# A fixed order on ScalarE and a fourth staging buffer in an attention and two-MoE kernel

## The chip, the cores and the metric

The kernel runs on one core of a Trainium2 chip. The metric is the device time of one execution in microseconds (us). A core has five engines that run their own instruction streams in order and meet through semaphores: TensorE (PE, matrix products and transposes; its weight loads are PEld), VectorE (DVE), ScalarE (ACT), GpSimd (POOL) and SyncE (SP, which issues most transfers).

## What is computed

Three stages, all in fp32: attention in a band of 64 positions (4 batches, 8 heads, 576 positions, head size 64), a dense layer pair with a squared relu (MoE1), and a layer pair for which each token picks one of eight experts (MoE2). Cut to what matters:

```python
scores = where((rel >= 0) & (rel < 64), q @ k.T / 8, -1e9)
x = (softmax(scores) @ v).reshape(2304, 512)

h = maximum(x @ w_in, 0)                 # 512 -> 2048
x = (h * h) @ w_out                      # 2048 -> 512

logits = x @ w_gate + modality_bias[modality_id]
e_idx = argmax(logits, 1); gate_w = softmax(logits)[e_idx]
for e in range(8):                       # tokens with e_idx == e
    out[mask] = gate_w * (maximum(x[mask] @ w1[e], 0) @ w2[e])   # 512 -> 1024 -> 512
```

## The kernel before

**Arithmetic.** An fp32 product is made of three matmul passes over operands that are split into a high and a low part: high by high, high by low, low by high. For every operand ScalarE makes the high part by a cast or by the activation itself (`xh` L769, `hh` L498 and L519, weights `w` L432) and VectorE the low part by a subtraction (`xl` L770, `hl` L506 and L520, weights L435). A matmul therefore waits for ScalarE first and for VectorE next.

**Steps.** `run` (L807 on) drives a job in steps. A step is one slice of the hidden layer: `emit_L1` issues its first-layer matmuls (L480), `evac_L1` brings the result from the accumulator to `hh` and `hl`, and then `emit_L2` issues the second-layer matmuls (L539) of the step before. In MoE1 `evac_L1` is a relu to `hr` (L492), a square to `hh` (L498), another square in place (L503) and the subtraction `hl`; in MoE2 it is one relu to `hh` (L519) and `hl`. Twice in a step `run` calls a `work` function, which inserts other work: half steps are numbered s = 0, 1, 2 and so on.

**Stages.** A hand-written program covers the attention and the first MoE1 groups. The last MoE1 group (512 tokens, 16 steps) is run with `last_work`. Then come units of 256 rows of MoE2: 0, 1 and 2 for the *guessed expert*, whose share of the first 14 token tiles is known early, then 3, a unit "w" of 384 rows, and 4 to 7. Units 0 and 1 have work functions of their own; from unit 2 on a loop over `seq` uses `u_work`.

**Weights.** `dma_chunks` (L391 on, the transfer at L399) lets SP load a 128 by 512 chunk (256 KB) of an expert's weights into a staging tile `st`; `split_steps` issues the cast of a chunk (L432), the subtraction of the chunk before, and the load of one more chunk. Sixteen chunks make a unit's weights. Staging has `nb` buffers (pool "stage2") for the guessed expert, issued in the last MoE1 group from half step `lsp` on, and `nb2` (pool "stage3") for those after it, whose memory is that of the gate's pool and so comes free after unit 1. The list `sp` says how many chunks are split in each half step of a unit.

**Gate.** `gate_steps` (L548 on) is done for each tile of 128 tokens. A copy `x` of MoE1's accumulator (L728, ScalarE) feeds eight dot products on VectorE (L559), the logits `nl` (L563), an exponential `lg` on ScalarE (L565), two small matmuls `ps_r` for the token's place in its expert's list, a scatter of the token's number into the table `tbl` (L588, POOL) and the write of its row to `xs` (L591, POOL). `slot(n)` issues the next n pieces of this and other background work.

**Rows of a unit.** `gather` reads a piece of the table into `ix` (L745), and POOL gathers the rows that it names (L751). `transp` transposes them on TensorE into `ps_x` (L310), from which `xh` and `xl` are made. At a unit's end ScalarE and VectorE scale the result `o` (L788, L790), and POOL scatters it to the output (L792).

**What sets the order.** The file fixes what is issued, but a scheduler chooses the order in which each engine meets its instructions, by times that it works out itself. It may move a weight cast ahead of an evacuation that the file has earlier, on any engine, within what data and buffers allow. Engines keep to the order chosen, however late one of its inputs may be.

Of the kernel before, what the change touches and what calls it, by code (L numbers as in the profile page):

```python
# [1 line left out]
KN = {'at1': ((0, 3, 4, 5), (3, 6, 7, 8), (6, 9, 10, 11), (9, 12, 13, 14)),  # L2
# [4 lines left out]

# [6 lines left out]
FP32 = mybir.dt.float32  # L14
F32R = mybir.dt.float32r
BF16 = mybir.dt.bfloat16
I32 = mybir.dt.int32
# [37 lines left out]
def kernel(  # L55
# [14 lines left out]
    nc = tc.nc  # L70
    NT, DM = out.shape
    E = w1.shape[0]
    NG = NT // 64
    NTT = NT // 128
# [9 lines left out]
    ROW = DM + 1  # L84
# [3 lines left out]
    const = ctx.enter_context(tc.tile_pool(name="const", bufs=1))  # L88
# [3 lines left out]
    small = ctx.enter_context(tc.tile_pool(name="small", bufs=2))  # L92
    dram = ctx.enter_context(tc.tile_pool(name="dram", bufs=1, space=DRAM))
    bank_p = ctx.enter_context(tc.tile_pool(name="bank", bufs=8, space=PSUM))
    att_ctx = ExitStack()
    att = att_ctx.enter_context(tc.tile_pool(name="att", bufs=2, side="right"))
    att2_ctx = ExitStack()
    att2 = att2_ctx.enter_context(tc.tile_pool(name="att2", bufs=1, side="right"))
    conv_ctx = ExitStack()
    conv = conv_ctx.enter_context(tc.tile_pool(name="conv", bufs=2))  # L100
    gp = {}
# [3 lines left out]
    tbl = dram.tile([NSLOT, 1], I32, name="tbl")  # L105

    ident = const.tile([128, 128], FP32, name="ident")
    maskn = const.tile([128, 128], FP32, name="maskn")
    mask_lo = const.tile([128, 128], FP32, name="mask_lo")
    mask_hi = const.tile([128, 128], FP32, name="mask_hi")  # L110
    upper = const.tile([128, 128], BF16, name="upper")
    ones = const.tile([128, 128], BF16, name="ones")
    row0 = const.tile([128, 128], BF16, name="row0")
# [70 lines left out]

    def setup_bias():
        nc.sync.dma_start(out=biasb, in_=mbias.partition_broadcast(128))
        modi = small.tile([128, NTT, 2], I32, tag="modi", name="modi", bufs=1)
        nc.sync.dma_start(out=modi, in_=mod)
        m1 = small.tile([128, NTT], FP32, tag="m1", name="m1", bufs=1)
        m0 = small.tile([128, NTT], FP32, tag="m0", name="m0", bufs=1)  # L190
        nc.vector.tensor_copy(m1, modi[:, :, 0])
        nc.vector.tensor_scalar(out=m0, in0=m1, scalar1=-1.0, scalar2=1.0, op0=ALU.mult, op1=ALU.add)
        tb = gp["x2"].tile([128, ROW], FP32, tag="x2", name="x2", bufs=4)[:, 0:NTT * E]
        tb = tb.rearrange("p (t e) -> p t e", e=E)
        for dst, m, r in ((bsel, m1, 1), (tb, m0, 0)):
            nc.vector.tensor_tensor(
                out=dst,
                in0=m.unsqueeze(2).to_broadcast([128, NTT, E]),
                in1=biasb[:, r, :].unsqueeze(1).to_broadcast([128, NTT, E]),
                op=ALU.mult,  # L200
            )
        nc.vector.tensor_tensor(out=bsel, in0=bsel, in1=tb, op=ALU.add)
# [3 lines left out]
    PRE = 6  # L206
# [3 lines left out]
    def home(kind, j):  # L210
        mine = held[kind]
        if j not in mine:
            mine[j] = att2 if j < PRE and not any(p is att2 for p in mine.values()) else att
        return mine[j]

    def load_qk(j):
# [174 lines left out]
    def dma_chunks(n):  # L391
        for _ in range(min(n, len(pend_dma))):
            key, c, f0, src = pend_dma.pop(0)
            w = src.shape[1]
            if len(src.shape) == 3:
                st = conv.tile([128, 512, 4], U16, tag="st", name="st", bufs=4)[:, 0:w, :]
            else:
                st = stage[0].tile([128, 512], FP32, tag="st", name="st", bufs=8 if stage[0] is conv else None)[:, 0:w]
            nc.sync.dma_start(out=st, in_=src)  # L399
            pend_split.append((key, c, f0, st))  # L400
# [28 lines left out]
    def split_hi(where, src):  # L429
        if where[0] not in units:  # L430
            units[where[0]] = ring.tile([128, 2, 4, 512], F32R, tag="w", name="w")
        nc.scalar.copy(out=part(where, 0, src), in_=src)  # L432

    def split_lo(eng, where, src):
        eng.tensor_tensor(out=part(where, 1, src), in0=src, in1=part(where, 0, src).bitcast(FP32), op=ALU.subtract)  # L435
        key, c, f0 = where
        done.update((key, c, f) for f in range(f0, f0 + src.shape[1], 256))

    def split_steps(n):
        for _ in range(n):  # L440
            if not pend_split and not pipe:
                return
            if pipe:
                split_lo(nc.vector, *pipe.pop())
            if pend_split:
                key, c, f0, st = pend_split.pop(0)
                pipe.append(((key, c, f0), st))
                split_hi(*pipe[0])
            dma_chunks(1)

    def add_expert(u, ev):
        for f in range(2):
            add_unit((u, "a", f), [
                w1[bass.ds(ev, 1), 128 * kk:128 * (kk + 1), 512 * f:512 * (f + 1)].rearrange("o p f -> (o p) f")
                for kk in range(4)])
            add_unit((u, "b", f), [
                w2[bass.ds(ev, 1), 512 * f + 128 * c:512 * f + 128 * (c + 1), :].rearrange("o p d -> (o p) d")
                for c in range(4)])
# [241 lines left out]
        yield  # L700


    bg = []

    def slot(n=1):
        for g in list(bg):
            while n > 0:
                try:
                    n -= 1
                    if next(g):  # L710
                        break
                except StopIteration:
                    n += 1
                    bg.remove(g)
                    break
# [22 lines left out]
    def gather(u, base, n):  # L738
        assert state["n"] >= (GUESS_TT if u in range(GUESS) else NTT)
        nh = 3 if u == "w" else 2  # L740
        sfx = "w" if u == "w" else ""
        pool = gp["wide"] if u == "w" else late["row"]
        ix = late["row"].tile([128, nh], I32, tag="ix" + sfx, name="ix" + sfx, bufs=1 if u == "w" else 3)
        eng = nc.gpsimd if u in range(GUESS) else nc.sync
        eng.dma_start(out=ix, in_=tbl[bass.ds(base, 128 * nh), :].rearrange("(h p) o -> p (h o)", p=128))  # L745
        r = []
        for hf in range(nh):
            t = pool.tile([128, ROW], FP32, tag="row", name="row")
            nc.gpsimd.memset(t, 1.0)
            ia = ix[:, hf:hf + 1].bitcast(U32)  # L750
            nc.gpsimd.indirect_dma_start(  # L751
                out=t[:, :], out_offset=None, in_=xs[0:n, :],
                in_offset=bass.IndirectOffsetOnAxis(ap=ia, axis=0),
                bounds_check=n - 1, oob_is_err=False)
            r.append((t, ia))
        rows[u] = r
# [96 lines left out]
    order = list(pend_dma)  # L853
# [99 lines left out]
    stage[0] = ctx.enter_context(tc.tile_pool(name="stage2", bufs=KN["nb"], side="right"))  # L953
    add_expert(0, ev0)

    def last_work(s):
        if s == 0:
            dma_chunks(KN["nb"])
        if s >= KN['lsp']:
            split_steps(1)  # L960
        slot(2)
        for u, at in enumerate(KN['lg']):
            if s == at:
                gather(u, bv0 + 256 * u, 128 * GUESS_TT)
# [31 lines left out]
    def prep(u):  # L996
        if u == "w":
            ew, bw = wei[0:1, 0:1], wbi[0:1, 0:1]
        else:
            ew, bw = ewi[0:1, u - GUESS:u - GUESS + 1], bsi[0:1, u - GUESS:u - GUESS + 1]  # L1000
        ev = nc.sync.value_load(ew, min_val=0, max_val=E - 1)
        evs[u] = nc.sync.value_load(bw, min_val=0, max_val=NSLOT - WIDE)
        add_expert(u, ev)
# [6 lines left out]
    def u_work(i, wide):  # L1010
        nxt = seq[i + 1] if i + 1 < len(seq) else None

        def f(s):
            if nxt is None or (wide and s % 2):
                return
            s = s // 2 if wide else s
            if s == KN['g']:
                gather(nxt, evs[nxt], NT)
            split_steps(KN['sp'][s])
            if s == KN['prep'] and i + 2 < len(seq):  # L1020
                prep(seq[i + 2])
                dma_chunks(KN["nb2"])
        return f

    def u_pieces(i, wide):
        def f(s):
            if i + 1 < len(seq) and s == (KN['tw_'] if wide else KN['t0'] if i == 0 else KN['t']):
                transp(seq[i + 1])
        return f

    for i, u in enumerate(seq):
        run(moe2_job(u), u_work(i, u == "w"), u_pieces(i, u == "w"), u == seq[-1])

    tot = nc.values_load(toti[0:1, 0:1], min_val=0, max_val=LIST)  # L1034

    def extra(u):
# [64 lines left out]
```

## Time and profile before

| | |
|---|---|
| median of 3 runs | 747.83 us (747.26 to 748.58) |
| profiled execution, its own time | 749.85 us |
| its span | 748.2 us |
| mean granted TensorE clock | 0.970 |
| TensorE busy | 700.5 us, 94% |
| VectorE, ScalarE, GpSimd busy | 448.2, 357.2 and 89.7 us (60%, 48%, 12%) |
| DMA | 84.49 MB in 62412 packets, mean 113 GB/s |

The times of the rows below are of the profiled execution, counted from its start. A wait is idle time of an engine together with what ended it. The granted clock is a share of TensorE's full 2.4 GHz. Busy time of matmuls is modelled and counts a slow matmul as busy too, so the loss behind a drop of the clock does not show as idle time. In this execution the last MoE1 group runs to about 508 us, unit 0 to about 531, unit 1 to about 554, and from there unit 2 and the rest follow.

### The profile page before, as it was taken

The numbers are of one execution on the slowest core, as the hardware profiler recorded it, in microseconds if no ns is written. First come the engines' busy times: TensorE is split into PE (matmuls) and PEld (weight loads), VectorE is DVE, ScalarE is ACT, GpSimd is POOL, SyncE is SP. The second block draws the span as 40 slices with busy tenths as digits, with TensorE's granted clock in tenths as the row PEclk, the third lists the DMA queues.
The fourth block names the chain that finished last, engine by engine and source line by source line (L and its number), as shares of the span: only waits on it lengthen the run. The fifth ranks groups of instructions, "written<-read, shape, count | busy, mean of one in ns | idle before, by whom it ended". The sixth has DMA issues, their size and how long they took to land. (4 is left out here: it accounts for less than half of the span.)

```text
span 748.2 us, 13360 instructions
## 1 busy us (share of the span) xinstructions
PE 700.5 (94%) x4777; PEld 599.1 (80%) x4777; DVE 448.2 (60%) x1394; ACT 357.2 (48%) x841; POOL 89.7 (12%) x126
## 2 busy tenths in 40 slices
PE   6499999999999999999999969799968999999995
PEld 5498888888888888788888757588868999999994
DVE  3999995597657433975446753118847765466311
ACT  5877667554444444553444333334106754456310
POOL 3000000000000000010001010400323321122111
PEclk7799999999999999999999999899988999999999
DMA  8976632435312203241201358400139874576200
GB/s 228 277 243 212 191 125 62 152 109 125 62 31 64 78 30 51 63 71 26 75 29 57 57 99 52 104 0 15 43 64 298 289 237 141 169 249 225 64 29 20
DMA packets 62412, 84.49 MB, mean 113 GB/s; under 512 B 26016, under 2 KB 35248, under 8 KB 62208
## 3 DMA queue, kind: packets, MB, share of 16 engines
q1 hardware_dynamic: 57136, 69.26, 34.9%
q0 software_dynamic: 5200, 14.29, 5.9%
q8 instruction: 39, 0.64, 0.4%
q14 instruction: 37, 0.30, 0.2%
HBM read 74.23 MB, written 9.82 MB: 112 GB/s over the span
## 5 line engine op out<-in xcount | busy, mean ns | idle before, releaser
L480 PE MATMUL l<-xh,w 128*128 128x256 f32 (+2 forms) x1344 | 318.2, 320 | 8.1 <-ACT xh L769 8.1
L539 PE MATMUL acc<-w,hh 128*128 128x512 f32 x880 | 280.4, 399 | 9.7 <-ACT hh L498 9.7
L480 PEld LDWEIGHTS l<-xh,w 128*128 128x128 f32 x1344 | 227.9, 191 | 27.9 <-ACT xh L769 8.8
L480 PE MATMUL l<-xl,w 128*128 128x256 f32 (+2 forms) x672 | 213.2, 317 | 0.0
L539 PEld LDWEIGHTS acc<-w,hh 128*128 128x128 f32 x880 | 161.9, 191 | 41.7 <-ACT hh L498 11.6
L539 PE MATMUL acc<-w,hl 128*128 128x512 f32 x440 | 174.5, 397 | 4.6 <-DVE hl L506 4.6
L480 PEld LDWEIGHTS l<-xl,w 128*128 128x128 f32 x672 | 128.4, 191 | 9.2 <-DVE xl L770 0.2
L539 PEld LDWEIGHTS acc<-w,hl 128*128 128x128 f32 x440 | 83.8, 190 | 26.1 <-DVE hl L506 8.2
L435 DVE TENSOR_TENSOR w<-st,w 128x512 fp32r<-128x512 f32 x112 | 72.3, 686 | 52.8 <-ACT w L432 52.7
L492 ACT ACTIVATE hr<-l 128x512 f32<-128x512 f32 x72 | 42.7, 593 | 122.1 <-PE l L480 108.7
L559 DVE CUSTOM_DVE_ANT_0 junk<-x,wgb 128x512 bf16<-128x512 f32 x144 | 98.9, 687 | 2.9 <-ACT x L728 0.4
L506 DVE TENSOR_TENSOR hl<-hr,hh 128x512 fp32r<-128x512 f32 x72 | 49.7, 690 | 83.0 <-ACT hr L503 82.6
L432 ACT CAST w<-st 128x512 fp32r<-128x512 f32 x112 | 64.2, 621 | 62.7 <-DMA st<-in_moe_w_dram 51.1
L277 ACT ACTIVATE p<-p,nm 128x128 f32<-128x128 f32 x144 | 55.9, 390 | 26.0 <-DVE nm L268 26.0
L519 ACT ACTIVATE hh<-l 128x512 fp32r<-128x512 f32 (+1 forms) x40 | 23.1, 577 | 82.8 <-PE l L480 76.4
L520 DVE SCALAR_TENSOR_TENSOR hl<-l,hh 128x512 fp32r<-128x512 f32 (+1 forms) x40 | 26.4, 660 | 53.0 <-ACT hh L519 52.9
L591 POOL DMA_DIRECT2D xs<-x x18 | 10.3, 572 | 308.0 <-PE ps_o L355 150.1
L498 ACT ACTIVATE hh<-hr 128x512 fp32r<-128x512 f32 x72 | 45.5, 631 | 3.2 <-PE acc L539 1.4
L503 ACT ACTIVATE hr<-hr 128x512 f32<-128x512 f32 x72 | 45.4, 631 | 1.7
L588 POOL DMA_INDIRECT tbl<-tid,pi x18 | 19.6, 1087 | 167.5 <-DVE pi L585 121.6
L310 PE MATMUL ps_t<-ident,p 128*128 128x128 f32 x144 | 23.6, 290 | 12.0 <-DVE p L302 9.0
L268 DVE CUSTOM_DVE_ANT_0 p<-ps_s,maskn 128x128 f32<-128x128 f32 x112 | 24.9, 285 | 11.9 <-POOL tri L175 6.4
(146 smaller groups left out, 559.6 us busy)
## 6 DMA issues: line engine op xcount, KB each, us to landing
st<-in_moe_w_dram SPq DMA_DIRECT2D x112, 256.0 KB, 4.0
vt<-in_v_dram SPq DMA_DIRECT2D x35, 256.0 KB, 3.8
st<-in_moe_w_out_dram SPq DMA_DIRECT2D x16, 512.0 KB, 3.7
kt<-in_k_dram SPq DMA_DIRECT2D x17, 384.0 KB, 3.9
st<-in_moe_w_in_dram SPq DMA_DIRECT2D x12, 512.0 KB, 4.9
xs<-x POOLq DMA_DIRECT2D x18, 256.5 KB, 3.8
qt<-in_q_dram SPq DMA_DIRECT2D x36, 128.0 KB, 4.4
st<-in_moe_w_in_dram SPq DMA_DIRECT2D x8, 256.0 KB, 5.2
```

The costliest lines, as they stand in the source:

```text
L268: nc.vector.tensor_tensor_reduce(out=p[:, pr, :], in0=ps[:, pr, :], in1=mk, scale=-SCALE, scalar=3.0e38, op0=ALU.add, op1=ALU.min, accum_o ...
L277: nc.scalar.activation(out=p[:, pr, :], in_=p[:, pr, :], func=ACTF.Exp, scale=-1.0, bias=nm[:, pr:pr + 1], accum_out=sm[:, pr:pr + 1])
L432: nc.scalar.copy(out=part(where, 0, src), in_=src)
L435: eng.tensor_tensor(out=part(where, 1, src), in0=src, in1=part(where, 0, src).bitcast(FP32), op=ALU.subtract)
L480: nc.tensor.matmul(out=ps[:, job.cols * j:job.cols * (j + 1)], lhsT=wt[:, a, kk, f0:f0 + 128], rhs=job.x[b][:, kk, :], start=(kk == 0 and ...
L492: nc.scalar.activation(out=e["r"], in_=ps, func=ACTF.Relu)
L498: nc.scalar.activation(out=e["hh"], in_=e["r"], func=ACTF.Square)
L503: nc.scalar.activation(out=e["r"], in_=e["r"], func=ACTF.Square)
L506: nc.vector.tensor_tensor(out=hl, in0=e["r"], in1=e["hh"].bitcast(FP32), op=ALU.subtract)
L520: nc.vector.scalar_tensor_tensor(out=hl, in0=ps, scalar=0.0, in1=hh.bitcast(FP32), op0=ALU.max, op1=ALU.subtract)
L539: nc.tensor.matmul(out=job.acc[th], lhsT=h[a][:, c0:c0 + 128], rhs=wt[:, b, c, :], start=(mp == 0 and j == 0 and n == 0), stop=(mp == last ...
L559: nc.vector.tensor_tensor_reduce(out=gp["junk"], in0=x2[:, 0:DM], in1=gp["wgb"][:, e, :], scale=1.0, scalar=0.0, op0=ALU.mult, op1=ALU.add ...
```

## The change

1. **Order.** The new functions `settle` and `skip` chain instructions of ScalarE to each other in the order of the file, by dependences that need no semaphore. The chain covers what is issued after `add_expert(0, ev0)`, that is from the last MoE1 group to the end of the loop over `seq`. The other engines are still ordered by the scheduler.
2. **Staging.** `nb` is 4 instead of 3. To make room, the masks of the attention move from the pool that lives throughout to one that ends with the attention.
3. **Pace.** Casts of the guessed expert begin at half step 8 instead of 7, and `last_work` issues one piece of background work instead of two from there on. The gathers of units 0 to 2 (`lg`) are two half steps later. From unit 2 on the casts are spread over all half steps (`sp0` for unit 2, `sp` for the others); the next unit but one is announced (`prep`) at half step 2 instead of 7, without loads at that place.
4. **Memory of the start.** The tile of the modality numbers shares a gate tile, which puts its load behind another one, and the value tiles of pair 4 and 5 change pools (`home`).

The core of the diff (list entries that stay are left out):

```diff
-      ... 'lsp': 7, 'lg': [20, 22, 24], ...
-      ... 'sp': [3, 3, 4, 4, 1, 3, 2, 0], 'nb': 3, 'nb2': 6, 'rb': 6, 'prep': 7, ...
+      ... 'lsp': 8, 'lg': [22, 24, 26], ...
+      ... 'sp0': [0, 1, 2, 2, 2, 3, 3, 4], 'sp': [2, 2, 2, 2, 2, 2, 2, 3], 'nb': 4, 'nb2': 6, 'rb': 6, 'prep': 2, ...
...
+    maskn, mask_lo, mask_hi = (att.tile([128, 128], FP32, name=n, bufs=1) for n in ("maskn", "mask_lo", "mask_hi"))
...
-    maskn = const.tile([128, 128], FP32, name="maskn")
-    mask_lo = const.tile([128, 128], FP32, name="mask_lo")
-    mask_hi = const.tile([128, 128], FP32, name="mask_hi")
...
-        modi = small.tile([128, NTT, 2], I32, tag="modi", name="modi", bufs=1)
+        tb = gp["x2"].tile([128, ROW], FP32, tag="x2", name="x2", bufs=4)
+        m1, m0 = (tb[:, NTT * k:NTT * (k + 1)] for k in (E, E + 1))
+        modi = tb[:, NTT * (E + 2):NTT * (E + 4)].bitcast(I32).rearrange("p (t w) -> p t w", w=2)
...
-            mine[j] = att2 if j < PRE and not any(p is att2 for p in mine.values()) else att
+            mine[j] = att2 if j < PRE and j != PRE - 2 and not any(p is att2 for p in mine.values()) else att
...
+    def settle(*engines):
+        made = nc.cur_bb.bb.instructions
+        for i in made[seen[0]:]:
+            if i.engine in engines:
+                if i.engine in tail:
+                    tc.add_manual_dep(i, tail[i.engine], mybir.DependencyInfo(
+                        mybir.DependencyClass.NoSync, mybir.DependencyReason.DATA), reason="order of the file")
+                tail[i.engine] = i.name
+        seen[0] = len(made)
+
+    def skip():
+        seen[0] = len(nc.cur_bb.bb.instructions)
+        tail.clear()
...
+    skip()
+    PINNED = (mybir.EngineType.Activation,)
...
-        slot(2)
+        slot(2 if s < KN['lsp'] else 1)
...
-            split_steps(KN['sp'][s])
+            split_steps(KN['sp' if i else 'sp0'][s])
             if s == KN['prep'] and i + 2 < len(seq):
                 prep(seq[i + 2])
-                dma_chunks(KN["nb2"])
...
+    settle(*PINNED)
```

Three places on ScalarE, the kernel before and the changed kernel one after the other. Line numbers of the changed kernel are its own: L489, L495 and L500 are relu, `hh` and second square, L429 the weight cast, L742 the copy of an accumulator, L562 the exponential, L516 the relu of MoE2, L783 `xh`, L802 the output scaling. First, the last MoE1 group where the casts of the guessed expert begin, before:

```order
L492 ACTIVATE hr<-l_4790 128x512
L432 CAST w<-st 128x512
L498 ACTIVATE hh<-hr 128x512
L432 CAST w<-st 128x512
L503 ACTIVATE hr<-hr 128x512
L432 CAST w<-st 128x512 x2
L492 ACTIVATE hr<-l_4846 128x512
L498 ACTIVATE hh<-hr 128x512
L565 ACTIVATE lg,gs<-nl,gm 128x8
L503 ACTIVATE hr<-hr 128x512
L432 CAST w<-st 128x512 x3
L492 ACTIVATE hr<-l_4904 128x512
```

and changed:

```order
L489 ACTIVATE hr<-l_4789 128x512
L495 ACTIVATE hh<-hr 128x512
L500 ACTIVATE hr<-hr 128x512
L429 CAST w<-st 128x512
L489 ACTIVATE hr<-l_4841 128x512
L495 ACTIVATE hh<-hr 128x512
L500 ACTIVATE hr<-hr 128x512
L429 CAST w<-st 128x512 x2
L489 ACTIVATE hr<-l_4895 128x512
L495 ACTIVATE hh<-hr 128x512
L500 ACTIVATE hr<-hr 128x512
L429 CAST w<-st 128x512 x2
```

Casts that stood between the relu, `hh` and the second square of a step now stand behind all three, one at first and then two for each step.

Second, the end of the last MoE1 group and unit 0, where `x` copies the accumulators of MoE1 for the gate, before:

```order
L769 CAST xh<-ps_x 128x4x128 x2
L728 COPY x_5449<-acc 128x512
L728 COPY x_5454<-acc 128x512
L519 ACTIVATE hh<-l_5417 128x512
L728 COPY x_5459<-acc 128x512
L728 COPY x_5464<-acc 128x512
L565 ACTIVATE lg,gs<-nl,gm 128x8
L519 ACTIVATE hh<-l_5481 128x512
L769 CAST xh<-ps_x 128x4x128 x2
L519 ACTIVATE hh<-l_5564 128x512
L565 ACTIVATE lg,gs<-nl,gm 128x8
```

and changed:

```order
L783 CAST xh<-ps_x 128x4x128 x2
L516 ACTIVATE hh<-l_5414 128x512
L742 COPY x_5446<-acc 128x512
L742 COPY x_5451<-acc 128x512
L742 COPY x_5456<-acc 128x512
L742 COPY x_5461<-acc 128x512
L562 ACTIVATE lg,gs<-nl,gm 128x8
L516 ACTIVATE hh<-l_5478 128x512
L783 CAST xh<-ps_x 128x4x128 x2
L562 ACTIVATE lg,gs<-nl,gm 128x8
L516 ACTIVATE hh<-l_5561 128x512
```

All four copies went behind the first `hh` of unit 0, and the second exponential went from behind the third `hh` to ahead of it.

Third, from unit 1 to unit 2, before:

```order
L519 ACTIVATE hh<-l_5861 128x512
L519 ACTIVATE hh<-l_5920 128x512
L432 CAST w<-st 128x512 x2
L769 CAST xh<-ps_x 128x4x128 x2
L432 CAST w<-st 128x512 x2
L788 ACTIVATE o<-acc,row 128x512
L432 CAST w<-st 128x512 x4
L519 ACTIVATE hh<-l_6031 128x512
```

and changed:

```order
L516 ACTIVATE hh<-l_5858 128x512
L516 ACTIVATE hh<-l_5917 128x512
L783 CAST xh<-ps_x 128x4x128 x2
L516 ACTIVATE hh<-l_6028 128x512
L802 ACTIVATE o<-acc,row 128x512
L429 CAST w<-st 128x512 x3
L516 ACTIVATE hh<-l_6095 128x512
L429 CAST w<-st 128x512 x4
```

The casts for unit 3 moved from both sides of `xh` to behind `xh`, the first `hh` of unit 2 and the output scaling.

## Rows read from the trace of the kernel before

**Rows 1.** Stages, core 0: window, its length, busy time (instructions) of each engine, granted clock, DMA share, GB/s

```profile
421.00:480.00 59.00, 46.00 (x182) 34.57 (x181) 24.82 (x78) 21.36 (x41) 11.79 (x13) 0.91 0.66 81
480.00:505.00 25.00, 25.00 (x112) 20.68 (x111) 2.77 (x4) 8.61 (x14) 1.50 (x2) 1.00 0.11 31
...
553.00:570.00 17.00, 8.88 (x47) 7.63 (x46) 6.19 (x10) 6.37 (x12) 3.52 (x6) 0.70 0.69 184
```

**Rows 2.** TensorE's waits, 420 to 480: total us, times, longest

```profile
PE acc L539 <- ACT hh L498: 9.7, 4, 4.7
PE acc L539 <- DVE hl L506: 3.3, 4, 1.3
```

**Rows 3.** Timeline of TensorE in the last MoE1 group: start, us, instruction, idle time before

```profile
413.00 0.39 PE L480 MATMUL l<-xh,w 128*128 128x512 f32 x1
...
447.18 0.73 PE L539 MATMUL acc<-w,hh 128*128 128x512 f32 x2 [3.84 <-ACT hh L498]
...
487.06 0.39 PE L480 MATMUL l<-xh,w 128*128 128x512 f32 x1
...
503.38 0.39 PE L480 MATMUL l<-xh,w 128*128 128x512 f32 x1
```

**Rows 4.** ScalarE's waits, 420 to 480

```profile
ACT w L432 <- DMA st<-in_moe_w_dram: 30.9, 6, 8.5
```

**Rows 5.** Timeline of ScalarE in the last MoE1 group

```profile
443.40 0.62 ACT L432 CAST w<-st 128x512 fp32r<-128x512 f32 x1 [8.46 <-DMA st<-in_moe_w_dram]
...
446.50 0.63 ACT L498 ACTIVATE hh<-hr 128x512 fp32r<-128x512 f32 x1
```

**Rows 6.** Timeline of TensorE between units 1 and 2

```profile
553.33 1.04 PE L310 MATMUL ps_x<-ident,row 128*128 128x128 f32 x8
...
563.41 0.58 PE L480 MATMUL l<-xh,w 128*128 128x256 f32 x1 [8.12 <-ACT xh L769]
```

**Rows 7.** Timeline of ScalarE between units 1 and 2

```profile
561.21 1.18 ACT L432 CAST w<-st 128x512 fp32r<-128x512 f32 x2 [9.84 <-DMA st<-in_moe_w_dram]
562.29 1.07 ACT L769 CAST xh<-ps_x 128x512 fp32r<-128x512 f32 x2
```

**Rows 8.** The table by stage (columns as in rows 1) behind the second hole

```profile
557.30:567.50 10.20, 4.09 (x14) 3.61 (x15) 5.08 (x9) 5.81 (x11) 1.88 (x3) 0.50 0.83 234
```

**Rows 9.** Weight loads (L399) issued in 399-416, 447-458 and 420-475

```profile
DMA to landing us min/median/max: 2.9/2.9/3.0
...
DMA to landing us min/median/max: 11.2/12.2/13.1
...
DMA to landing us min/median/max: 2.6/7.8/13.1
```

**Rows 10.** Timeline of POOL in the last MoE1 group

```profile
447.78 1.01 POOL L588 DMA_INDIRECT tbl<-tid,pi  x1 [0.31 <-issue]
457.99 1.03 POOL L588 DMA_INDIRECT tbl<-tid,pi  x1 [9.20 <-issue]
```

**Rows 11.** Timeline of ScalarE in unit 0

```profile
508.10 0.59 ACT L728 COPY x<-acc 128x512 f32<-128x512 f32 x1
...
522.21 0.60 ACT L519 ACTIVATE hh<-l 128x512 fp32r<-128x512 f32 x1 [2.15 <-PE ps_r L575]
523.35 0.30 ACT L565 ACTIVATE lg<-nl,gm 128x8 f32<-128x8 f32 x1 [0.54 <-DVE gm L563]
```

**Rows 12.** Timeline of TensorE in unit 0, the first L2 matmul of its third step

```profile
527.73 0.71 PE L539 MATMUL acc<-w,hh 128*128 128x512 f32 x2
```

**Rows 13.** Timeline of POOL, third row gather for unit "w"

```profile
590.68 1.02 POOL L751 DMA_INDIRECT row<-xs,ixw  x1 [0.30 <-issue]
```

**Rows 14.** Timeline of TensorE, transposes for unit "w"

```profile
604.32 1.47 PE L310 MATMUL ps_x<-ident,row 128*128 128x128 f32 x12
```

**Rows 15.** Weight loads (L399) issued in 553 to 700

```profile
DMA to landing us min/median/max: 2.4/3.9/6.4
```

**Rows 16.** ScalarE's waits, 553 to 748

```profile
ACT w L432 <- DMA st<-in_moe_w_dram: 20.2, 13, 9.8
```

More of the change, by code (lines that the diff above doesn't have):

```diff
@@ L186, in setup_bias @@
         nc.sync.dma_start(out=biasb, in_=mbias.partition_broadcast(128))
-        modi = small.tile([128, NTT, 2], I32, tag="modi", name="modi", bufs=1)
+        tb = gp["x2"].tile([128, ROW], FP32, tag="x2", name="x2", bufs=4)
+        m1, m0 = (tb[:, NTT * k:NTT * (k + 1)] for k in (E, E + 1))
+        modi = tb[:, NTT * (E + 2):NTT * (E + 4)].bitcast(I32).rearrange("p (t w) -> p t w", w=2)
         nc.sync.dma_start(out=modi, in_=mod)
-        m1 = small.tile([128, NTT], FP32, tag="m1", name="m1", bufs=1)
-        m0 = small.tile([128, NTT], FP32, tag="m0", name="m0", bufs=1)
         nc.vector.tensor_copy(m1, modi[:, :, 0])
         nc.vector.tensor_scalar(out=m0, in0=m1, scalar1=-1.0, scalar2=1.0, op0=ALU.mult, op1=ALU.add)
-        tb = gp["x2"].tile([128, ROW], FP32, tag="x2", name="x2", bufs=4)[:, 0:NTT * E]
-        tb = tb.rearrange("p (t e) -> p t e", e=E)
+        tb = tb[:, 0:NTT * E].rearrange("p (t e) -> p t e", e=E)
         for dst, m, r in ((bsel, m1, 1), (tb, m0, 0)):
@@ L700, in list_steps @@
         yield
+    seen, tail = [0], {}
+    def settle(*engines):
[10 more added lines that the diff above has]
+        tail.clear()
     bg = []
```

4 rows, old and new, of the table KN are left out of this document.

## The prediction

> **What bounds the kernel now.** I read the table by stage first, then TensorE's waits in the stages where its busy time falls short of the stretch, then the engine that those waits name. From 480 to 505 us TensorE is busy the whole time at full clock; in the two stretches 421 to 480 and 553 to 570 it is busy 46.00 of 59.00 us at a mean clock of 0.91 and 8.88 of 17.00 us at 0.70 [rows 1]. Between them and after them TensorE waits for nothing that the list of waits shows. So the kernel is bound by TensorE, with two holes in it, and a change that only moves ScalarE's work and weight loads can be worth those holes and no more.
>
> *The first hole.* TensorE waits there for `hh` (9.7 us) and for `hl` (3.3 us), the two halves of MoE1's hidden tile [rows 2]. How much the hole costs in all is better read from the pace than from the waits, since the clock falls too. The last matmul of L1 starts at 413.00 in the third step of the last group and at 503.38 in the last, thirteen steps later; the last three steps, which are free of waits, take (503.38 - 487.06) / 3 = 5.44 us each [rows 3]. Thirteen such steps are 70.7 us, the rows give 90.4: **19.7 us** are lost. What ScalarE did meanwhile: six times it stood before a cast of the guessed expert's weights whose staged tile had not landed, 30.9 us in all [rows 4]. One such place shows the link: the cast at 443.40 had waited 8.46 us, the square that makes `hh` came behind it at 446.50 [rows 5], and TensorE's L2 matmul began at 447.18 after 3.84 us idle [rows 3].
>
> *The second hole.* After the transposes for unit 2 at 553.33, L1 starts only at 563.41, 8.12 us of it a wait for `xh` [rows 6]. ScalarE ran two weight casts ahead of that `xh`, and the casts had waited 9.84 us for their loads [rows 7]. Behind the idle time the granted clock is 0.50 (the 1.2 GHz level) in the stretch 557.3 to 567.5, with 4.09 us of matmuls in it [rows 8], half of which, 2.0 us, is the lower clock's. That makes 8.1 + 2.0; of it some 0.5 us stay in any order, since `xh` itself takes 1.07 us for its two casts [rows 7] behind the transposes. **9.7 us** can be had.
>
> Both holes have one cause: a cast that is not urgent was put ahead of work that is, on an engine that runs in order. The floor of the change is therefore 19.7 + 9.7 = 29.4 us.
>
> **The change, part by part.**
>
> *Order in the last MoE1 group.* With ScalarE in the written order each step's relu and two squares stand ahead of that step's casts, one cast per half step of 2.72 us, so a late load delays the next step's `hh` at the earliest. ScalarE's own work is no limit: three passes of 0.63 and two casts of 0.62 us [rows 5] are 3.1 us of 5.44. A cast's load is issued when the cast four places ahead has run (three before). Four places are 4 x 2.72 = 10.9 us, and the next step's `hh` has another 3 to 4 us before L2 needs it (a step is L1, 2.7 us, and the L2 of the step before, 2.7 us), so a load may take about 14.5 us from issue to landing; with three buffers it would be 11.8. The loads issued from 420 to 475 took 2.6 to 13.1 us with a median of 7.8; the slowest, issued between 447 and 458, took 11.2 to 13.1 [rows 9]. All fit in 14.5, three would not have fitted well in 11.8. So both parts are needed, and together they are enough by 1.4 us. The slow ones lie beside the scatters of the gate's table, which POOL issued at 447.78 and 457.99, the second after 9.20 us of waiting for the first to be done [rows 10]; loads issued from 399 to 416 took 2.9 to 3.0 [rows 9]. I take all of 19.7, less 0.6 for one `hl` that comes behind a run of the gate's dot products on VectorE: **-19.0**, bounds -9.7 (the slack is short and half the stalls stay) and -19.7.
>
> That rests on the row and against a rule. The Trainium skill, page "DMA: Bandwidth & Descriptors", section "Queues, rings and completion order", says that each DMA engine goes round its queues packet by packet. By that a load beside a scatter of small packets would be held up little, and land in about 3 us as the undisturbed ones do; the late-weights rival below would have no chance, and this term would stand at its floor. The measured 13.1 us speak against it, and the measurement decides.
>
> *Order in units 0 and 1.* Here written order costs something, because before there is no wait. The four copies of MoE1's last accumulators, of which the first ran at 508.10 [rows 11], stand behind `hh` of unit 0's first step now, some 4 us later; the gate of tiles 14 to 17 waits for them, and VectorE's dot products with it. The exponential `lg` of tile 15, which ran at 523.35 behind `hh` at 522.21 [rows 11], now stands ahead of that `hh`. With the gate 3.9 us later it ends at about 527.6, `hh` at about 528.3, `hl` a pass later at about 529, and L2 wants them from 527.73 [rows 12]: **+1.6**, bounds 0 (the gate catches up on VectorE) and +4 (it does not, and the next exponential is late too).
>
> *Unit 1 to unit 2.* The casts stand behind `xh`, `hh` and the output scaling now. `xh` comes right behind the transposes: **-9.7**. What is late next: the first three casts stand ahead of the second step's `hh`, and their loads can't be issued earlier than now, since their buffers lie where the gate's tiles were. The first landed shortly before 561.21 [rows 7]; even 3 us later, three casts and the relu end by 567, and that `hh` is wanted about 569, as a step of L1 and L2 lies between. Bounds -9.7 and -6.
>
> *Gathers.* POOL's third row gather for unit "w", issued at 590.68 [rows 13], moves behind a scatter of unit 2's output and its index load waits for a paced cast: I put it some 2.6 us later. Its transposes, at 604.32 [rows 14], come some 8 us earlier by the terms above. A landing of 5 to 6 us puts the rows at about 598 to 599, against transposes at about 597: **+1.2**, bounds 0 and +3. The steadier pace of casts in units 2 to 7 costs nothing as long as loads land as they do (2.4 to 6.4 us, median 3.9 [rows 15]). Moving the masks, the modality load and value pair 4 touches the attention phase, where TensorE is fed from elsewhere; I take 0, bounds -1 and +1.
>
> Sum: -19.0 + 1.6 - 9.7 + 1.2 = **-25.9 us**. The profiled execution's own 749.85 us (span 748.2) becomes about 724; the median of the runs shown lies 2.0 us under that execution, so it becomes 747.8 - 25.9 = **722**.
>
> **The rivals.**
>
> *Late weights keep part of the first hole.* Written order turns a late load into a late `hh` directly, with no scheduler to go round it. Four loads in flight at 13.1 us each are one per 3.3 us, against a demand of one per 2.72; twelve casts at that rate fall 7 us behind, and every stall is followed by matmuls at the lower clock, half as much again: 10 us of 19.7 stay, 732, and with unit 2's first loads late as well 740. For it: the landings of 11.2 to 13.1 [rows 9]. Against: those are three of thirteen loads.
>
> *Nothing is gained.* If the loads are late by bandwidth and not by order, both holes stay and move: 747 to 748. Against: loads without a scatter land in 3 to 4 us [rows 9, 15].
>
> *Slower.* In units 2 to 7 casts that still wait for loads stand ahead of `hh` now. Before, the casts from unit 2 on waited 20.2 us in thirteen places [rows 16], without a wait of TensorE but the one above. If written order passed these on, and the first hole stayed at its 19.7, the time would be 747.8 - 9.7 + 20.2 = 758. The point where it decides: two casts per step of 2.9 us are one per 1.45 us, six buffers cover a landing of 8.7 us. The rows show 6.4 at most [rows 15], so it is unlikely.
>
> *All new waits vanish.* Without +1.6 and +1.2, and with -19.7: 718.5, or a little less.
>
> **How the numbers follow.** Both holes close with a few us of new waits (717 to 728): 0.66. Late weights (728 to 742): 0.20. Better than 717: 0.06. No difference: 0.03. Slower: 0.05. The range 716 to 734 leaves out most of the last two, the upper part of the late weights and the far end below. A difference of 0.2%, 1.5 us, is about what a measurement of this kernel can tell from none: faster 0.92, same 0.03, slower 0.05.
>
> **What would show it.** In the profile after: steps of 5.44 us through the last group, and no wait of TensorE for `hh` over 1 us there; casts one by one behind the second square; `xh` of unit 2 within 2 us of its transposes; granted clock 1.00 in both stretches. A wait for `hh` in unit 0 of 1 to 2 us and one for rows before unit "w" would bear out the added terms. Wrong would be: waits for staged weights above 15 us in the last group with `hh` behind them, a clock of 0.50 there again, or waits for `hh` in units 2 to 7.

## The result, and the profile after

The changed kernel takes 735.6 us (median of 4 runs, 734.75 to 736.96) where the kernel before takes 748.0 (747.26 to 748.58): ratio 0.9826, 95% interval 0.9811 to 0.9841. That is 12.4 us faster. 25.9 us were forecast, and 735.6 lies 1.6 us above the forecast range. The profiled execution takes 735.87 us, its span is 734.2.

The table by stage of the changed kernel (window, its length, busy time with instructions of PE, PEld, DVE, ACT, POOL, granted clock, DMA share, GB/s) answers to [rows 1]:

```profile
421.00:480.00 59.00, 59.00 (x266) 48.40 (x265) 32.43 (x102) 30.00 (x55) 11.74 (x13) 1.00 0.53 75
...
553.00:570.00 17.00, 10.93 (x55) 8.96 (x55) 10.33 (x18) 8.99 (x17) 5.84 (x6) 0.80 0.79 255
```

The last MoE1 group has become a solid block: 59.00 busy us of 59.00 at full clock, where before there were 46.00 at 0.91. The later stretch still has a hole, though, and it is another one. TensorE's waits from 395 us on (total us, times, longest), against [rows 2, 6]:

```profile
PE ps_x L307 <- DMA row<-xs,ix: 6.2, 3, 5.4
PE ps_x L307 <- DMA row<-xs,ixw: 1.1, 1, 1.1
```

No wait for `hh` or for `xh` is left in this list. TensorE waits for gathered rows now: those of unit 3 and, a little, those of unit "w". ScalarE's wait for staged weights in the last group fell from the 30.9 us of [rows 4] to

```profile
ACT w L429 <- DMA st<-in_moe_w_dram: 2.8, 4, 1.4
```

The order of TensorE's matmuls is almost the same in both kernels. So one can take the same matmul, by its number in that order, in both timelines and see how much sooner it starts; the difference between two such places is what a stage gained or lost, to some 0.3 us. The places are the matmuls number 3100, 3300, 3600, 3700, 3800, 4000 and 4776 (counted from 0, so that 4776 is the last). In the kernel before they start at 428.73, 492.50, 541.99, 567.72, 582.33, 613.19 and 739.79.

| us, after minus before | start to last group | last MoE1 group | units 0, 1 | entry of unit 2 | rows of unit 3 | rows of "w" | rest | sum |
|---|---|---|---|---|---|---|---|---|
| forecast | 0 | -19.0 | +1.6 | -9.7 | 0 | +1.2 | 0 | -25.9 |
| measured | +2.6 | -19.0 | +0.9 | -10.4 | +8.6 | +1.8 | +1.6 | -14.0 |

The sum of -14.0 is that of the two profiled executions; the medians differ by 12.4. Both holes were filled as forecast, to 0.7 us. Then most of the second gain was handed back 20 us later. The chain can be read in three views of the changed kernel. SyncE issued six weight loads, then the index of unit 3, then nothing until 551.87:

```profile
541.52 3.95 SPq L396 DMA_DIRECT2D st<-in_moe_w_dram  x6
546.91 0.38 SPq L759 DMA_DIRECT2D ix<-tbl  x1
551.87 21.45 SPq L396 DMA_DIRECT2D st<-in_moe_w_dram  x19
```

GpSimd issued the last table scatter at 539.83, and could not gather the rows before the index was there:

```profile
539.83 1.00 POOL L585 DMA_INDIRECT tbl<-tid,pi  x1 [6.68 <-DVE xl L784]
541.45 1.46 POOL L763 MEMSET row<- 128x513 f32 x3 [0.63 <-DMA xs<-x]
554.82 1.12 POOL L765 DMA_INDIRECT row<-xs,ix  x1 [11.91 <-DMA ix<-tbl]
556.25 1.22 POOL L765 DMA_INDIRECT row<-xs,ix  x1 [0.31 <-issue]
```

TensorE began the last matmul of its L2 step at 556.04 and then stood before the transposes:

```profile
556.04 0.39 PE L536 MATMUL acc<-w,hl 128*128 128x512 f32 x1
561.84 1.08 PE L307 MATMUL ps_x<-ident,row 128*128 128x128 f32 x4 [5.42 <-DMA row<-xs,ix]
563.45 1.11 PE L307 MATMUL ps_x<-ident,row 128*128 128x128 f32 x4 [0.53 <-DMA row<-xs,ix]
564.22 0.56 PE L477 MATMUL l<-xh,w 128*128 128x256 f32 x1
```

From its issue at 546.91 the index took 7.1 us to land, the two gathers took 6.9 and 7.2. In the kernel before the index took 2.8 us and each gather 4.6, with a margin that the second hole had given them. The POOL timeline of the kernel before:

```profile
569.49 1.07 POOL L751 DMA_INDIRECT row<-xs,ix  x1 [2.10 <-issue]
570.86 1.04 POOL L751 DMA_INDIRECT row<-xs,ix  x1 [0.30 <-issue]
```

and TensorE's:

```profile
581.11 1.03 PE L310 MATMUL ps_x<-ident,row 128*128 128x128 f32 x8
```

The first rows landed at 569.49 + 4.6 = 574.1, and the transposes came at 581.1: 7.0 us of slack. In the changed kernel TensorE reaches them 9.2 us sooner on the same count (556.04 and the 0.23 of one matmul, plus 15.6, is 571.9 against 581.1; 15.6 us is the lead that it had at matmul 3600). So 2.2 us of the wait are simply the slack used up. The rows themselves come at 561.84 + 15.6 = 577.4 on that count, 3.3 us later than before: the gather was issued 0.9 us later (554.82 + 15.6 against 569.49) and took 2.3 us longer (6.9 against 4.6). 2.2 + 3.3 is the wait of 5.4 to 0.1. The rest of the 8.6 us lies around it. TensorE's lead falls from 26.0 us at matmul 3700 to 24.8 just ahead of the transposes, most of it at the second `hh` of unit 2 (552.39), which stood behind three casts whose loads came late; behind the wait come the second wait and the lower clock (0.55 from 562.5 to 566).

### The profile page after: what moved, and what is told of

It reads as the page before. It is cut to its first block, busy times and chain, and to the rows that moved or that the text cites. A ratio compares the mean times of both kernels' runs of the same rounds, so it can differ in the third digit from the quotient of the medians.

```text
span 734.2 us, 13351 instructions
## 1 busy us (share of the span) xinstructions
PE 699.3 (95%) x4777; PEld 599.7 (82%) x4777; DVE 448.4 (61%) x1394; ACT 356.8 (49%) x841; POOL 89.7 (12%) x126
## 5 line engine op out<-in xcount | busy, mean ns | idle before, releaser
L536 PE MATMUL acc<-w,hh 128*128 128x512 f32 x880 | 277.2, 395 | 0.0
L536 PEld LDWEIGHTS acc<-w,hh 128*128 128x128 f32 x880 | 160.0, 188 | 30.8 <-ACT hh L495 0.4
L536 PE MATMUL acc<-w,hl 128*128 128x512 f32 x440 | 172.3, 392 | 2.4 <-DVE hl L503 2.2
L489 ACT ACTIVATE hr<-l 128x512 f32<-128x512 f32 x72 | 42.7, 593 | 127.8 <-PE l L477 110.8
L432 DVE TENSOR_TENSOR w<-st,w 128x512 fp32r<-128x512 f32 x112 | 72.1, 685 | 16.6 <-ACT w L429 16.4
L429 ACT CAST w<-st 128x512 fp32r<-128x512 f32 x112 | 63.8, 618 | 15.4 <-DMA st<-in_moe_w_dram 15.0
L516 ACT ACTIVATE hh<-l 128x512 fp32r<-128x512 f32 (+1 forms) x40 | 23.0, 574 | 82.5 <-PE l L477 82.5
L588 POOL DMA_DIRECT2D xs<-x x18 | 10.3, 574 | 304.4 <-DVE lg L556 145.9
L495 ACT ACTIVATE hh<-hr 128x512 fp32r<-128x512 f32 x72 | 45.5, 632 | 3.5 <-PE acc L536 1.5
L500 ACT ACTIVATE hr<-hr 128x512 f32<-128x512 f32 x72 | 45.5, 632 | 1.9
L307 PEld LDWEIGHTS ps_t<-ident,p 128*128 128x128 f32 x144 | 18.0, 149 | 17.0 <-ACT p L274 12.7
```

Of the source, the lines that this page charges most:

```text
L307: nc.tensor.transpose(out, in_, ident)
L489: nc.scalar.activation(out=e["r"], in_=ps, func=ACTF.Relu)
L495: nc.scalar.activation(out=e["hh"], in_=e["r"], func=ACTF.Square)
L500: nc.scalar.activation(out=e["r"], in_=e["r"], func=ACTF.Square)
L536: nc.tensor.matmul(out=job.acc[th], lhsT=h[a][:, c0:c0 + 128], rhs=wt[:, b, c, :], start=(mp == 0 and j == 0 and n == 0), stop=(mp == last ...
```

## The experiments

Each kernel here was timed beside the kernel before on the same chip. That took 749.2 us on the chip of e1 to e4, 749.7 on that of e5 to e8 and 753.8 on that of e8b and e9, so ratios are compared rather than times. The stage table for all of them, us against the one profile of the kernel before, follows. Its columns are stretches, whatever is lost in them: in e7 and e9 most of what stands under "rows 3" is a wait for `hh` and what follows it.

| kernel | start | last group | units 0, 1 | entry of 2 | rows 3 | rows "w" | rest | sum | ratio (95%) |
|---|---|---|---|---|---|---|---|---|---|
| changed | +2.6 | -19.0 | +0.9 | -10.4 | +8.6 | +1.8 | +1.6 | -14.0 | 0.9826 (0.9811-0.9841) |
| e1 index first | +3.2 | -19.0 | +0.9 | -10.4 | +1.7 | +8.6 | +2.2 | -12.8 | 0.9811 (0.9778-0.9844) |
| e2 unit 0 free | +0.9 | -19.0 | +0.5 | -10.4 | +2.6 | +1.8 | +1.4 | -22.2 | 0.9716 (0.9686-0.9747) |
| e3 three buffers | +0.3 | -18.5 | +0.9 | -10.4 | +7.9 | +2.2 | +2.2 | -15.4 | 0.9803 (0.9776-0.9829) |
| e4 order free | +0.6 | -17.8 | +0.5 | +0.2 | +0.3 | +0.1 | +1.1 | -14.9 | 0.9816 (0.9790-0.9843) |
| e5 pace only | +1.4 | -6.2 | +0.4 | -0.5 | +0.7 | +0.1 | +1.2 | -2.9 | 1.0002 (0.9979-1.0024) |
| e6 before, buffers | +2.0 | -19.0 | +0.4 | -0.8 | +0.2 | +0.1 | +1.1 | -15.9 | 0.9828 (0.9802-0.9854) |
| e7 before, order | -0.6 | -14.3 | +0.8 | -10.4 | +10.3 | 0.0 | +1.5 | -12.7 | 0.9873 (0.9848-0.9898) |
| e8 indices early, unit 0 free | +2.3 | -19.0 | +0.4 | -10.4 | +0.7 | +0.1 | +2.0 | -23.8 | 0.9699 (0.9669-0.9729) |
| e8b, the same again | +4.6 | -19.0 | +0.5 | -10.4 | +0.5 | +0.1 | +1.5 | -22.2 | 0.9668 (0.9652-0.9685) |
| e9 indices early, order fixed | +4.6 | -19.0 | +0.9 | -10.4 | +5.6 | +0.1 | +1.1 | -17.1 | 0.9737 (0.9712-0.9762) |

### What made the rows of unit 3 late

Two theories. Q: the index load stands behind six weight loads in SyncE's queue. G: the gate of tiles 14 to 17 is late since ScalarE's copies are pinned behind `hh`, which puts the last table scatter at 539.83 instead of 550.36 - 15.6 = 534.8, 5 us late.

**e1** moves the index load ahead of the weight loads:

```diff
     prep(seq[1])
+    gather(seq[1], evs[seq[1]], NT)
     dma_chunks(KN["nb2"])
...
-            if s == KN['g']:
+            if s == KN['g'] and i:
```

> The changed kernel with one move: the index load of unit 3 is issued by SP ahead of the six weight loads for that unit instead of behind them; every other engine keeps its order. Theory Q (queue): in the changed kernel this index load took 7.1 us because it stood behind six loads of 256 KB, where before it took 2.8. It expects the index to land within 3.5 us of its issue, TensorE's wait for the gathered rows (5.4 + 0.5 us) to shrink to 2 us or less with little or nothing at half clock behind it, and 735.6 - 6 = about 729.5 us (728 to 732). Rival G (gate): the index is late because the gate of tiles 14 to 17 is late, and its issue at 546.9 can't move; it expects the wait to stay at 4 us or more and 734 to 736 us.

Measured: 736.03 us, no gain, where Q expected 728 to 732. But the index landed 2.1 us after its issue, and the wait for unit 3's rows all but went, as Q said. The wait turned up one unit later. TensorE's waits from 395 us on in this kernel:

```profile
PE ps_x L307 <- DMA row<-xs,ixw: 5.2, 3, 2.2
PE ps_x L307 <- DMA row<-xs,ix: 1.6, 2, 0.8
```

and the queue of SyncE shows why:

```profile
546.45 0.39 SPq L759 DMA_DIRECT2D ix<-tbl  x1
547.19 24.74 SPq L396 DMA_DIRECT2D st<-in_moe_w_dram  x25
572.10 0.38 SPq L759 DMA_DIRECT2D ixw<-tbl  x1
```

The index of unit "w" stands behind twenty-five weight loads, which began 5.7 us later than in the changed kernel. It is issued only 1.4 us sooner (572.10 against 573.49) for a TensorE that is there about 6 us sooner. So Q was right that the queue holds the index up and wrong on the price: moving one index alone buys nothing.

**e2** leaves unit 0 to the scheduler, which brings two copies and the exponentials back to where they were:

```diff
+    settle(*PINNED)
     run(moe2_job(0), u0_work, u_next(0))
+    skip()
```

> The changed kernel, but in unit 0 ScalarE is left to the scheduler: two of the four copies of MoE1's accumulators and the exponentials go back to where they stood in the kernel before. Rival G: the pinned copies made the last table scatter some 5 us later relative to TensorE's work; it expects that scatter, the index and the rows 4 us earlier, the wait for rows at 2 us or less, and about 730 us (728 to 732). Theory Q: the index still lands about 7 us after its issue since six loads stand ahead of it; if the loads start earlier too, the gain comes all the same, so what tells the two apart is the landing time: 7 us by Q, under 4 by a G that does without the queue. If neither matters: 735 to 736.

Measured: 728.11 us, 7 to 8 us better than the changed kernel. GpSimd's timeline has the last scatter 7.8 us sooner, and the rows with it:

```profile
532.01 0.99 POOL L585 DMA_INDIRECT tbl<-tid,pi  x1 [4.20 <-DVE sa L687]
...
547.70 1.23 POOL L765 DMA_INDIRECT row<-xs,ix  x1 [8.68 <-DMA ix<-tbl]
```

2.1 us of the 7.8 are the earlier part of this execution (0.9 instead of 2.6 at the start, 0.4 in units 0 and 1). The index still landed 4.9 us after its issue at 541.96, behind its six loads, which is neither the 7 us of Q nor the under 4 of G. The landings of the loads explain it. The last load ahead of the index landed at 553.8 in the changed kernel (issued at 545.14, 8.7 us), at 546.7 in e2 and at 568.1 in the kernel before; the index followed at 554.0, 546.9 and 568.4, each time 0.2 to 0.3 us later. So what counts is how long the loads ahead of it take. They took 8.5 to 9.0 us in the changed kernel, where all six were issued (541.5 to 545.1) before the last table scatter had landed (546.7), and 5.4 to 5.8 in e2, where only the first (537.6) was issued before that (538.5). Both theories hold a part: the wait is a sum of the late gate, the queue, slower gathers, and the slack that is gone.

**e8** does both, for both indices: unit 0 free as in e2, and

```diff
     prep(seq[1])
+    prep(seq[2])
+    gather(seq[1], evs[seq[1]], NT)
+    gather(seq[2], evs[seq[2]], NT)
     dma_chunks(KN["nb2"])
...
-            if s == KN['g']:
+            if s == KN['g'] and i > 1:
...
-            if s == KN['prep'] and i + 2 < len(seq):
+            if s == KN['prep'] and i and i + 2 < len(seq):
```

> The changed kernel with unit 0 left to the scheduler and with the index loads and row gathers of both unit 3 and unit w issued at the start of unit 2, ahead of all weight loads for unit 3. Theory C (two index loads stand late in SP's order, behind six and behind twenty-five weight loads that the paced casts and the bandwidth hold up; moving one alone only moved the wait to the other): no wait of TensorE for rows above 0.5 us at either place, 728.1 less the 4.4 us that the two waits and the lower clock behind them cost: 722 to 725. Rival W (the weight loads, which come 5 us later for it and share the engines with five row gathers, are late themselves): waits for hh or for weights in units 2 and 3, 727 to 733.

Measured: 726.03 us, ratio 0.9699, the shortest time of all. That is 1 us above the expected range; the start of the profiled execution took 2.3 us more than in the kernel before, and in the stages the expectation was right: 0.7 and 0.1 us left. All of TensorE's waits from 395 us on:

```profile
PE ps_x L307 <- DMA row<-xs,ix: 0.4, 2, 0.2
```

SyncE's queue has the two indices first, and forty-two weight loads behind them without harm:

```profile
540.52 0.39 SPq L759 DMA_DIRECT2D ix<-tbl  x1
541.08 0.38 SPq L759 DMA_DIRECT2D ixw<-tbl  x1
541.88 45.68 SPq L396 DMA_DIRECT2D st<-in_moe_w_dram  x42
```

**e9 and e8b** ask how much of that needs the free unit 0. e9 is e8's edit of the indices on the changed kernel, with its order fixed everywhere; e8b is e8 again on the same chip.

> The changed kernel, order fixed everywhere, with the index loads and row gathers of unit 3 and unit w both issued at the start of unit 2 (the edit of the run before, without freeing unit 0). It tells how much each half of that version is worth. If the late gate of units 0 and 1 still matters once the index loads stand first, a wait of 1 to 2 us for the rows of unit 3 stays, as in the run that moved that one index load alone, with nothing at unit w, and unit 0 costs its 0.9 us: 727 to 730 us. If the queue was all: 725 to 727.

> The version with unit 0 free and both index loads early, again, on the chip of the run beside it: 724 to 728 us. It is here so that the two are compared under the same conditions, and for a second reading of what the attention phase takes, which has differed by up to 3 us between profiled executions of the same instructions.

Measured: 733.44 (ratio 0.9737) against 728.76 (0.9668). The free unit is worth 0.7%, 5 us, and not as I had expected by a wait for rows. TensorE waits for `hh` in e9:

```profile
PE acc L536 <- ACT hh L516: 2.9, 1, 2.9
```

On ScalarE of e9 the second `hh` of unit 2 stands behind three casts, whose loads begin at 549.17 behind the late indices:

```profile
552.20 0.62 ACT L429 CAST w<-st 128x512 fp32r<-128x512 f32 x1 [5.55 <-DMA st<-in_moe_w_dram]
553.47 0.62 ACT L429 CAST w<-st 128x512 fp32r<-128x512 f32 x1 [0.65 <-DMA st<-in_moe_w_dram]
556.78 0.62 ACT L429 CAST w<-st 128x512 fp32r<-128x512 f32 x1 [2.69 <-issue]
557.30 0.59 ACT L516 ACTIVATE hh<-l 128x512 fp32r<-128x512 f32 x1
```

That is the mechanism of the prediction's rival "Slower": a late load ahead of `hh` in a fixed order. It happens once the loads start 7 us later than in e8, 4.6 of them on TensorE's count. The four kernels form a square. Over the two columns of rows the changed kernel loses 10.4 us, with unit 0 free alone (e2) 4.4, with the indices first alone (e9) 5.7, with both (e8) 0.8.

### Which part of the change filled the first hole

The prediction said that order and fourth buffer are both needed. **e3** has three buffers,

```diff
-      ... 'nb': 4, ...
+      ... 'nb': 3, ...
```

and **e4** no fixed order:

```diff
-    settle(*PINNED)
     tot = nc.values_load(toti[0:1, 0:1], min_val=0, max_val=LIST)
```

> The changed kernel with three staging buffers for the guessed expert's weights instead of four, order and pace as changed. By the working of the prediction a load may then take about 11.8 us from issue to landing, and loads beside a table scatter took 11.2 to 13.1: it expects one or two waits of TensorE for hh in the last MoE1 group, 1 to 6 us in all, 737 to 742 us. Rival (the order alone closes the hole): no wait there, 735 to 737.

> The changed kernel without the fixed order: ScalarE is left to the scheduler everywhere, with four buffers, the new pace and the new places of the start. By the theory that the order closes the holes: casts stand between relu, hh and square again and two of them ahead of unit 2's xh; the first hole returns in part (four buffers start loads earlier, so 8 to 16 of its 19 us), the second whole (8 to 10 us), and the wait for rows goes since TensorE comes later: 743 to 752 us. Rival (the fourth buffer alone closes the first hole): 735 to 740.

Measured: 735.04 and 735.48 us, both like the changed kernel. Both expectations were wrong, and in both the rival was right: either part can go. The last group keeps -18.5 and -17.8. In e3 ScalarE's waits in 420 to 480 have

```profile
ACT w L429 <- DMA st<-in_moe_w_dram: 9.8, 3, 5.8
```

and TensorE's longest wait there is 0.2 us: casts do come late, but behind the work that matters. In e4 casts stand between relu, `hh` and square again, and they wait for

```profile
ACT w L429 <- DMA st<-in_moe_w_dram: 8.0, 4, 4.8
```

8.0 us instead of 30.9, and TensorE waits 0.7 us in that stretch: the loads are there in time. e4 also has the second hole back, whole, and none of the late rows:

```profile
PE l L477 <- ACT xh L783: 8.2, 1, 8.2
PE acc L536 <- DVE hl L503: 0.7, 1, 0.7
```

So from unit 0 to the end e4 loses 2.2 us on the kernel before and the changed kernel 2.5 (the sums of the columns behind the last group). The fixed order on ScalarE bought 10.4 us at the entry of unit 2 and paid them back within two units.

e3 and e4 left open whether the new pace alone would do, so three more: **e5** has the edits of e3 and e4 together, so the pace and the moves at the start are what is left. **e6** is the kernel before with the moves at the start (masks, modality tile, value pairs) and

```diff
-      ... 'nb': 3, ...
+      ... 'nb': 4, ...
```

**e7** is the kernel before with `settle` and `skip` as in the change, and nothing else:

```diff
     add_expert(0, ev0)
+    skip()
+    PINNED = (mybir.EngineType.Activation,)
...
+    settle(*PINNED)
     tot = nc.values_load(toti[0:1, 0:1], min_val=0, max_val=LIST)
```

> The changed kernel with neither the fixed order nor the fourth buffer: only the new pace and the new places of the start are left of the change. Both runs with one of the two parts taken out kept the first hole closed, so: theory E (either of the two is enough, neither is not): the first hole returns, 10 to 19 us, beside the second hole of 8 to 10 us, 745 to 752 us with ScalarE waiting 20 us or more for staged weights in the last MoE1 group. Rival P (the new pace is what closes it: casts start a half step later and background work comes in single pieces): ScalarE waits under 12 us there, TensorE under 2, and the time is that of the run with the order free, 735 to 738.

> The kernel before with the fourth buffer and the memory moves that make room for it, old pace, order free. Theory E: the buffer alone closes most of the first hole, TensorE waits 4 us or less in the last MoE1 group, the second hole stays: 730 to 738. Rival P: without the new pace the hole stays at 10 us or more: 742 to 750.

> The kernel before with the fixed order alone: three buffers, old pace. Theory E: the first hole closes to 4 us or less, the second closes (-10), and the rows of unit 3 come late as in the changed kernel (+3 to +9): 726 to 738. Rival P: with the old pace (casts a half step earlier, two background pieces per half step) hh stands behind casts that wait for loads, 5 us or more stay in the first hole: 738 to 746.

Measured: 749.65, 736.16 and 739.68 us. Theory E holds in e5 and e6; e7 came out between E and rival P. The pace alone recovers 6.2 us of the first hole and leaves 12.8, with 25.4 us of ScalarE's waits for weights, and in time it brings nothing (ratio 1.0002). TensorE's waits in e5 from 395 us on:

```profile
PE l L477 <- ACT xh L783: 7.5, 1, 7.5
PE acc L536 <- ACT hh L495: 6.8, 2, 5.1
PE acc L536 <- DVE hl L503: 2.1, 3, 1.3
```

The buffer alone recovers all 19.0 and is as fast as the whole change (0.9828 against 0.9826). The order alone recovers 14.3 and leaves 4.7, more than the 4 of theory E and less than the 5 of P; its time lies above E's 738 and in P's range. So the pace has a share where the order works with three buffers: with it 18.5 are recovered (e3). With the old pace a fixed order also hurts in unit 2, where TensorE waits for `hh` longer than for rows:

```profile
PE acc L539 <- ACT hh L519: 5.1, 1, 5.1
PE ps_x L310 <- DMA row<-xs,ix: 2.3, 2, 1.3
PE acc L539 <- ACT hh L498: 1.8, 1, 1.8
PE acc L539 <- DVE hl L506: 1.7, 3, 0.7
PE acc L539 <- ACT w L432: 1.2, 1, 1.2
```

## Why the prediction was right and wrong

**The first hole: right in size.** -19.0 forecast, -19.0 measured; the working by steps of 5.44 us held. Wrong was "both parts are needed": the buffer alone does it (e6), the order alone most of it (e7), with the new pace nearly all of it (e3). "Both holes have one cause" is too simple as well: in e4 casts stand ahead of `hh` as before, and the first hole is closed, since the loads are there in time. It took a cast put ahead and a late load together. The mis-sized term is the landing of loads. 14.5 us of room with four buffers and 11.8 with three were held against 11.2 to 13.1 us, the slowest of [rows 9]; in the changed kernel the slowest took 10.6 (loads issued from 420 to 475: 2.6, 6.0 and 10.6 us least, median and most), and in e3 9.5 (all sixteen). So three buffers fit too. Why the slowest loads landed sooner there, no run separates. The slow landings stay far above the 2.9 us of undisturbed loads, as the measurement in the prediction had it.

**Units 0 and 1: right in sign.** +1.6 forecast, +0.9 measured, about 0.4 of it by the pinned order (e2, with unit 0 free, has +0.5, and e6, with no pinned order at all, +0.4). The gate was indeed later, the exponential of tile 15 by about 3.5 us on TensorE's count, but the `hh` behind it started at 511.01 and came just in time; the wait for `hh` in unit 0 that was named as a sign did not come.

**The second hole: right.** -9.7 forecast, -10.4 measured.

**What is late next: the step that failed.** In "Unit 1 to unit 2" I asked what would be late next and named the casts ahead of the second `hh`. It was the rows of unit 3. They have no term in the sum at all: "Gathers" prices the third gather of "w" and nothing else. The trace of before gives their slack, 7.0 us, and the same part of the prediction takes 9.7 us off TensorE's way to them. That alone should have opened the term. The gate's delay, which I had priced only for its effect on `hh`, and the index behind six loads make it 5.4 us of wait, and 8.6 us of time in that stretch. The casts that I did ask about cost under 1 us of these. With the second hole still open there is no such wait (e4, e6: +0.3 and +0.2), and with scatter and index early 0.4 us of it are left (e8: +0.7).

**Gathers of "w": the number by luck.** +1.2 forecast, +1.8 measured, 1.1 us of it a wait. But the working behind +1.2 was a third gather 2.6 us later and transposes 8 us sooner. In the changed kernel they are

```profile
583.00 1.03 POOL L765 DMA_INDIRECT row<-xs,ixw  x1 [0.30 <-issue]
...
587.45 1.03 PE L307 MATMUL ps_x<-ident,row 128*128 128x128 f32 x8
```

With the 16.4 us of TensorE's lead at the end of the last group, against [rows 13, 14], the gather came 8.7 us later and the transposes 0.5 us sooner: the late rows of unit 3 had held both back, and the two errors cancel. In e2, where that wait is small, the working holds: 2.0 us later (574.61), 7.2 sooner (579.06), a wait of 1.4.

**The attention phase: not settled.** 0 forecast, +2.6 measured in the profiled pair. But e1 to e6, e8, e8b and e9 have the same engines' orders through the attention phase, and their starts lie between +0.3 and +4.6; on one chip alone, e1 to e4, between +0.3 and +3.2. So most of the +2.6 can be scatter between executions. e7, with the old start, has -0.6 in one profile. What the moves at the start cost within that scatter was not measured.

**The rest: open.** 0 forecast, +1.6 measured. Every kernel of the table has +1.1 to +2.2 there, those with the order free too (e4, e6). No run shows the cause.

**The rivals.** "Late weights", at 732 and with a late unit 2 740, had a time near the one measured and not its cause: the last group has no wait of TensorE, and late loads cost under 1 us in unit 2. "Slower" did not come in the changed kernel, but for that 1 us; its mechanism showed in e9 and e7. The forecast's range went wrong for want of a rival in which filling the second hole uncovers the gather behind it.

## What to carry to other kernels

An idle stretch of the bounding engine is also slack for every chain that runs beside it. Before its removal is booked as a gain, the landing of each input that this engine needs next is to be set against the new arrival time, and not only the inputs that the moved instructions touch. Small loads on which a chain hangs, such as an index, belong ahead of bulk loads on a queue, provided that they can be issued by then: in e9 the index that was not ready yet held back the loads behind it, and `hh` waited 2.9 us. And a fixed order on one engine should be checked for which of the waits that it moves lies in front of work that another engine needs.

## What the runs showed of the hardware

An index of 1 KB took 2.1 us when it was issued ahead of the weight loads (e1) and 7.1 us behind six of 256 KB (changed kernel), from the same queue. In three profiles it landed 0.2 to 0.3 us after the last load ahead of it, whether that took 3.1 us (before), 5.5 (e2) or 8.7 (changed kernel). The Trainium skill, "DMA: Bandwidth & Descriptors", section "Queues, rings and completion order", says that each DMA engine takes the descriptors of one queue row in ring order; these numbers agree with that.

Profiled executions with the same instructions at the start differ on one chip by 2.9 us at the end of the attention phase (e3 +0.3, e1 +3.2), and the chip of e8b and e9 was slower in that phase (+4.6 for both) and in the whole of the kernel before (753.8 us). The place of a gain of a few us is told better by stages than by whole times.
